# MoE 2 in two passes over the groups of weights, with seven products for all four blocks of tokens

## The chip, the cores and the metric

The kernel runs on one core of one Trainium2 chip. The metric is the device time of one execution in microseconds (us), as the median of three runs. Engines are named as in the profile: PE (TensorE), PEld (its weight loads), DVE (VectorE), ACT (ScalarE), POOL (GpSimd) and SP (SyncE, which issues most of the DMAs).

## The reference

Three stages, one after the other: attention with rotary embedding over 4 batches, 8 heads, 576 positions and 64 channels; a feed-forward stage with a clipped gate ("MoE 1"); a second one with a sigmoid gate ("MoE 2"). Both have 2304 tokens, 512 channels inside and out and 2048 hidden units. Their weights come as float64, all else as float32.

```python
attn = softmax(rotate(q) @ rotate(k).T / 8) @ v
x = attn.transpose(0, 2, 1, 3).reshape(2304, 512)
h = x @ w_in;  x = (h * clip(h + 3, 0, 6) / 6) @ w_out                 # MoE 1
h = x @ w_in2; out = (h / (1 + exp(-1.702 * h))) @ w_out2              # MoE 2
```

## The kernel before

Every matrix product is made of three: each float32 operand is split into a high part that the matmul's fp32r type holds and a low rest, and high x high, high x low and low x high are summed in PSUM. The splitting is a copy (`copy`, L399, most often on ACT) for the high part and a subtraction (`sub`, L389, on POOL or DVE) for the low one.

The order of all instructions is made by a planner (`Plan`, L81). `plan.op` (L94) notes an operation with its engine (and others that may take it), a cost, a key, and the buffers that it reads and writes. `plan.run` (L152) simulates the engines: whenever one is free it takes the ready operation with the lowest key whose buffers can be had, and the order that comes out is the order in which each engine's instructions stand in the program. Keys are thus priorities, spoken in planned time; an operation with a late key runs early if its engine has nothing else to do. The constants of the planner are in `C` (L31). On the chip every engine, SP's and POOL's DMA queues too, works its list in that order. The kernel calls `plan.run` three times: for attention with MoE 1 of batches 0 to 2 (L922), for the rest of MoE 1 and the start of MoE 2 (L954), and for MoE 2 (L1154).

Attention runs pair of heads by pair of heads (`pair`, L433), 16 in all. The probabilities are transposed on PE (L611) and split (L615, L632) for the product with v (L638). For some of them, as `full` (L417) says, the product is made in plain fp32 with v itself (L628), which saves the DVE's subtraction. MoE 1 of one batch (`moe1`, L766; 512 tokens, the last call also the 4 x 64 tail tokens) runs beside the attention of the next. Both feed-forward stages go over 8 groups of 256 hidden units (G = 2 slices of 128). The tokens form five blocks: 0 to 3 are the first 512 tokens of each batch, 4 holds the 256 tail tokens.

A group's weights are made by `weights` (L685). Kind "f64" loads pieces of 512 float64 per partition ("raw", two buffers), converts each to float32 ("cvt", two buffers) with one ACT instruction (L719), one POOL instruction (L721) and two DVE instructions (L725, L728), and splits it into high and low (wih, wil, woh, wol, two buffers each). In MoE 1 the first batch does this and stores the halves in DRAM ("keep", `w1_hl`), and the later batches load them through POOL's queue (kind "split", L695).

MoE 1's results of batches 0 to 2 go to DRAM (`y_dram`, L912) and come back near the end of MoE 1 (L934). Scaled by 1/6 they are split into yh and yl, one pair of buffers for each of the five blocks (L942 to L952).

MoE 2's order is `seq` (L962): per group the blocks 0, 2, 1, 3, 4, and behind each block's input products the output products of the block before. There are two forms of input products:

- "h" (L1016): per slice of 128 units 12 matmuls of 512 columns (256 for block 4), a sigmoid on ACT (L1033), a product on DVE (L1035), and the split into gh and gl.
- "w" (L1040), for blocks 0 and 1 from the second group on: units, channels and tokens are each cut in two, and seven products take the place of the eight products of halves, by sums of weight blocks (sh, sl; L736 to L758, made per group in buffers of the tags woh and wol) and of token blocks (th, tl; `ysums`, L986, once). The seven products are 42 matmuls of 256 columns (L1067) in four PSUM banks; one ACT copy (L1082) and four DVE additions (L1084 to L1090) recombine them into "hw" (one buffer), then sigmoid, product (L1103) and split.

"o" (L1107) are the output products of 128 tokens: six matmuls of 512 columns (L1139), added by DVE (L1143, L1145) into `oacc`, which holds all tokens; the last group's results are stored by SP (L1149; the tail's in halves, L1127). Weights of every group are converted from float64 within MoE 2 (L1010 to L1012).

## Time and profile before

| | before |
|---|---|
| median of three runs | 1136.02 us (1135.9 to 1136.06) |
| the profiled execution | 1136.14 us |
| span of the profiled execution, first to last instruction | 1134.3 us |
| granted TensorE clock, mean | 0.996 |
| PE / DVE / ACT / POOL busy | 97 / 63 / 49 / 57% of the span |

Times of stages, instructions and waits below are from the profiled execution. Starts are in us from its first instruction. A matmul's end is modelled, and matmuls overlap in the pipeline; its cost to the stream is the distance from its start to the next one's start. The profile writes "woh" for the sums' buffers too, since they share its tag, and w_hl for `w1_hl`.

### The profile page before, as it was taken

To read this page: it belongs to the slowest core of one execution; us is meant where nothing else is said; L and a number is where in the kernel's file an instruction comes from. 1 tells how busy PE (TensorE), PEld (TensorE's weight loads), DVE (VectorE), ACT (ScalarE), POOL (GpSimd) and SP (SyncE) were. 2 spreads that over 40 slices of the span, in tenths; PEclk is the share of its full clock that TensorE was granted. 3 is DMA by queue.
4 is the path that set the end of the run, shared out by engine and by line. 5 is a ranking of instruction groups with operands and counts; after the bars stand their busy time and mean duration, and the time that the engine had idled before them with its cause. 6 is when DMAs were issued, how large, how long until landed. Compare 5 with 4: busy or idle time off the path is not lost.

```text
span 1134.3 us, 16742 instructions
## 1 busy us (share of the span) xinstructions
PE 1098.7 (97%) x6264; PEld 898.2 (79%) x6264; DVE 713.2 (63%) x1092; ACT 558.9 (49%) x1133; POOL 645.3 (57%) x640
## 2 busy tenths in 40 slices
PE   5999999999999999999999999999999999999995
PEld 4666777777888888878887888888888888888884
DVE  5788777877656665566664544655655655566543
ACT  5788766666755564655556412444323433333330
POOL 5875876969563477363326435466645647455440
PEclk9999999999999999999999999999999999999998
DMA  3434565656543545443337543122102011120012
GB/s 92 129 129 142 160 225 165 212 183 206 171 130 111 153 151 181 120 141 107 112 112 260 157 140 85 66 74 75 42 34 75 19 56 37 39 74 21 19 75 93
DMA packets 58888, 129.69 MB, mean 114 GB/s; under 512 B 13752, under 2 KB 26808, under 8 KB 58040
## 3 DMA queue, kind: packets, MB, share of 16 engines
q1 hardware_dynamic: 44712, 78.13, 21.4%
q0 software_dynamic: 13824, 50.34, 14.7%
q8 instruction: 49, 0.80, 0.3%
q14 instruction: 31, 0.25, 0.1%
q10 hardware_dynamic: 272, 0.16, 0.0%
HBM read 103.97 MB, written 24.64 MB: 113 GB/s over the span
## 4 chain that ended last, share of the span: by engine, by line
PE 92%; DVE 5%; ACT 1%; issue 0%; DMA 0%; SPq 0%; DVEq 0%; ACTq 0%
PE psum L839 17%; PE psum L1139 17%; PE psum L814 17%; PE psum L1027 11%; PE psum L1067 6%; PE psum L611 6%; PE psum L558 5%; PE psum L638 4%; PE psum L628 3%; PE psum L598 1%; PE psum L545 1%; DVE sc L531 1%; DVE cvt L728 1%; PE psum L498 1%; PE psum L580 1%; PE psum L623 1%
## 5 line engine op out<-in xcount | busy, mean ns | idle before, releaser
L391 POOL TENSOR_TENSOR gl<-t,gh 128x512 fp32r<-128x512 f32 (+1 forms) x144 | 184.4, 1284 | 138.0 <-ACT gh L401 118.9
L533 ACT ACTIVATE P<-psum,sc 128x576 f32<-128x576 f32 x144 | 105.5, 739 | 60.4 <-DVE sc L531 60.0
L531 DVE TENSOR_REDUCE sc<-psum 128x1 f32<-128x576 f32 x144 | 102.6, 752 | 35.4 <-PE psum L558 31.8
L1145 DVE TENSOR_TENSOR oacc<-oacc,psum 128x512 f32<-128x512 f32 x124 | 85.0, 686 | 48.9 <-PE psum L1139 47.4
L615 ACT ACTIVATE PTh<-psum 128x512 fp32r<-128x512 f32 (+2 forms) x160 | 89.0, 598 | 49.3 <-PE psum L611 48.0
L1139 PE MATMUL psum<-woh,gh 128*128 128x512 f32 x284 | 111.2, 392 | 0.0
L1139 PE MATMUL psum<-woh,gl 128*128 128x512 f32 x284 | 110.8, 390 | 0.0
L1139 PE MATMUL psum<-wol,gh 128*128 128x512 f32 x284 | 110.7, 390 | 0.0
L401 ACT ACTIVATE gh<-t 128x512 fp32r<-128x512 f32 (+1 forms) x134 | 81.1, 607 | 53.3 <-DVE t L1035 25.7
L814 PE MATMUL psum<-xh,wih 128*128 128x512 f32 x256 | 105.7, 413 | 1.5 <-DVE t L821 1.2
L839 PE MATMUL psum<-gh,woh 128*128 128x512 f32 x256 | 104.3, 407 | 0.1
L848 DVE TENSOR_TENSOR y<-y,psum 128x512 f32<-128x512 f32 x112 | 76.4, 685 | 42.5 <-PE psum L839 41.7
L814 PE MATMUL psum<-xh,wil 128*128 128x512 f32 x256 | 100.5, 393 | 0.0
L839 PE MATMUL psum<-gh,wol 128*128 128x512 f32 x256 | 100.4, 392 | 0.0
L814 PE MATMUL psum<-xl,wih 128*128 128x512 f32 x256 | 100.3, 392 | 0.0
L839 PE MATMUL psum<-gl,woh 128*128 128x512 f32 x256 | 100.2, 391 | 0.0
L821 DVE SCALAR_TENSOR_TENSOR t<-t,psum 128x512 f32<-128x512 f32 (+1 forms) x80 | 50.0, 631 | 68.2 <-ACT t L819 68.0
L611 PE MATMUL psum<-ident,P 128*128 128x128 f32 (+1 forms) x640 | 87.9, 275 | 2.7 <-ACT P L533 1.2
L611 PEld LDWEIGHTS psum<-ident,P 128*128 128x128 f32 (+1 forms) x640 | 71.6, 135 | 23.6 <-issue 4.7
L819 ACT ACTIVATE t<-psum,three 128x512 f32<-128x512 f32 (+1 forms) x80 | 50.7, 644 | 79.8 <-PE psum L814 62.4
L1035 DVE TENSOR_TENSOR t<-t,psum 128x512 f32<-128x512 f32 (+1 forms) x52 | 31.5, 606 | 78.3 <-ACT t L1033 68.1
L632 DVE TENSOR_TENSOR PTl<-psum,PTh 128x512 fp32r<-128x512 f32 x92 | 61.5, 685 | 29.0 <-ACT PTh L615 28.7
(193 smaller groups left out, 2936.7 us busy)
## 6 DMA issues: line engine op xcount, KB each, us to landing
raw<-in_moe_w_in_dram SPq DMA_DIRECT2D x32, 512.0 KB, 3.8
raw<-in_moe_w_out_dram SPq DMA_DIRECT2D x32, 512.0 KB, 3.6
wih<-w_hl POOLq DMA_DIRECT2D x24, 512.0 KB, 4.4
wil<-w_hl POOLq DMA_DIRECT2D x24, 512.0 KB, 5.2
woh<-w_hl POOLq DMA_DIRECT2D x24, 512.0 KB, 4.4
wol<-w_hl POOLq DMA_DIRECT2D x24, 512.0 KB, 5.0
...
```

Source lines behind the costliest of these rows:

```text
L391: alts = [("Pool", ns or gps(n), lambda: nc.gpsimd.tensor_tensor(o(), i0(), i1(), op=op)), ("DVE", dve(n), lambda: nc.vector.tensor_tensor ...
L401: alts = {"ACT": ("ACT", act(n, psum), lambda: nc.scalar.activation(o(), i(), AF.Copy, scale=scale)), "DVE": ("DVE", dve(n, not psum), lam ...
L531: plan.op("DVE", dve(S), key + C["oM"], lambda: nc.vector.tensor_reduce(sc.t[:, i:i + 1], Sp.t[:, :, :HS], axis=AX.XY, op=ALU.max, negate= ...
L533: plan.op("ACT", act(S, True, True), key + C["oE"], lambda: nc.scalar.activation(halves(P[i].t), Sp.t[:, :, :HS], AF.Exp, bias=sc.t[:, i:i ...
L611: nc.tensor.transpose(T.t[:m, 0, c * 128:c * 128 + 128], P[hs + c].t[:, j * 128:j * 128 + m], ident)
L615: plan.op("ACT", act(512, True), key + C["oTh"], lambda T=T, hi=hi, m=m, fp=fp: nc.scalar.activation(hi.t.bitcast(F32) if fp else hi.t[:m] ...
L814: nc.tensor.matmul(hp.t[:, 0, :n], ww.t[:, cc, fs], xx.t[:, cc, :n], start=(cc == 0 and i == 0), stop=(cc == CC - 1 and i == 2))
L839: nc.tensor.matmul(yp.t[:, 0, :n], ww.t[:, a, cs], xx.t[:, a, :n], start=(i == 0), stop=(i == 3 * G - 1))
L848: plan.op("DVE", dve(n), ka + C["oY"], lambda yp=yp, y=y, c=c, n=n: nc.vector.tensor_tensor(y.t[:, c, :n], y.t[:, c, :n], yp.t[:, 0, :n], ...
L1027: nc.tensor.matmul(hp.t[:, 0, :n], ww.t[:, cc, fs], xx.t[:, cc, :n], start=(cc == 0 and i == 0), stop=(cc == CC - 1 and i == 2))
L1139: nc.tensor.matmul(op_.t[:, 0], xx.t[:, ts], ww.t[:, a, :], start=(i == 0), stop=(i == 3 * G - 1))
L1145: plan.op("DVE", dve(512), key, lambda op_=op_, tt=tt: nc.vector.tensor_tensor(oacc.t[:, tt], oacc.t[:, tt], op_.t[:, 0], op=ALU.add), r=[ ...
```

## The change

- **Two passes.** Pass 0 runs over all eight groups for the blocks 0, 1 and 4, pass 1 again over all groups for 2 and 3. Blocks 0 to 3 use the form "w" in every group, the first too; block 4 stays "h".
- **Operands.** Each of blocks 0 to 3 has seven prepared token operands in buffers of 7 x 512 (`prep`). Blocks 0 and 1 are prepared near the end of MoE 1; 2 and 3 within MoE 2 (`later`), 3 in block 0's buffers. y of batch 3 goes to DRAM too.
- **Weights.** Pass 0 makes the halves and the sums and stores all six in `w2_hl`; pass 1 loads them through POOL's queue. In pass 0 the sums have one pair of buffers (sh, sl); pass 1 alternates between these and block 4's.
- **Conversion.** The float64 conversion is moved out into `chunk`. For groups 0 to 4 (GZ = 5) it is planned into the first `plan.run`, in 20 chunks with keys Z0 + Z1 * i, and stored as float32 in `w2_f`; pass 0 loads these (kind "f32"). Groups 5 to 7 convert in pass 0 as before.
- **Buffers.** `oacc` is split by blocks, 2 and 3 reuse those of 0 and 1; hw has two buffers, gh2 and gl2 five each.
- **Order of the seven products** is 1, 2, 4, 6, 5, 7, 3 (before 1, 2, 6, 5, 7, 3, 4); the last store in two halves is block 3's last 128 tokens.
- **Constants.** F11 (unsplit products in batch 1, second head) goes from 3 to 2; keys of attention, MoE 1 and the planner's margins MA and MP change.

```diff
-C = {'T0': 59.504, 'D1': 12.604, 'LN1': 168.009, 'LN2': 130.306, 'LN3': 403.413, 'LM': 383.596, 'X': 32.498,
-     'K0': 3.856, 'RQ': 21.006, 'RK': 17.07, 'TQ': 1.889, 'TK': 1.171, 'V': 1.427, 'PB': 11, 'RT': 1.0, 'oM':
-     -0.122, 'oE': 0.391, 'REC': 1.0, 'TT': 1.191, 'TH': 0.258, 'TS': 0.034, 'PV': 1.449, 'PTB': 6, 'oTh':
-     0.144, 'oTl': -0.485, 'WL': 1.78, 'WS': 4.551, 'WS2': 1.346, 'MD': 8000, 'MA': 2000, 'MP': 400, 'YB':
-     1.149, 'YB0': -2.222, 'YS': 0.858, 'YT': -0.851, 'W2L': 22.0, 'W2S': 13.7, 'W2S2': -11.5, 'HC': 0.255,
-     'HD': -0.23, 'YD': 1.226, 'SPX': -9.638, 'F00': 3, 'F01': 1, 'F10': 2, 'F11': 3, 'F20': 0, 'F21': 0, 'G0':
-     5, 'T8': 0.572, 'P8': -1.224, 'SE': 1, 'MODE': 0.5, 'PORT': 8.0, 'oR': 0.2, 'oS': 1.092, 'oG': 9.844,
-     'oGl': -3.864, 'oY': -2.295, 'WC': -0.306}
+YBB = 1
+GZ = 5
+C = {'T0': 5.556, 'D1': 16.553, 'LN1': 168.009, 'LN2': 130.306, 'LN3': 403.413, 'LM': 383.596, 'X': 32.498,
+     'K0': 3.862, 'RQ': 18.769, 'RK': 18.355, 'TQ': 1.955, 'TK': 0.488, 'V': 1.136, 'PB': 11, 'RT': 1.0, 'oM':
+     -0.161, 'oE': 0.181, 'REC': 1.0, 'TT': 1.191, 'TH': 0.258, 'TS': 0.034, 'PV': 1.449, 'PTB': 6, 'oTh':
+     0.135, 'oTl': -0.478, 'WL': 1.803, 'WS': 4.642, 'WS2': 1.809, 'MD': 8000, 'MA': 8000, 'MP': 1000, 'YB':
+     1.048, 'YB0': -1.916, 'YS': 0.962, 'YT': 0.207, 'W2L': 22.0, 'W2S': 13.7, 'W2S2': -11.5, 'HC': 0.255, 'HD':
+     -0.141, 'YD': 1.283, 'SPX': -10.726, 'F00': 3, 'F01': 1, 'F10': 2, 'F11': 2, 'F20': 0, 'F21': 0, 'G0': 7,
+     'T8': 0.572, 'P8': -1.553, 'A0': 33.259, 'A1': 18.273, 'A2': 1.936, 'Z0': 406.045, 'Z1': 43.053, 'SE': 1,
+     'MODE': 0.5, 'PORT': 8.0, 'oR': 0.196, 'oS': 2.726, 'oG': 9.077, 'oGl': -6.999, 'oY': -3.913, 'WC': -0.237}
...
+    def chunk(nm, w, g, z, t_load, after=()):
...
+        return t
...
+                if sums and nm == "wi":
+                    d["sh"], d["sl"] = [Buf(plan, y3pool, x, [128, CC, 256], F32R, 1) for x in (("yh4", "yl4"), ("sh", "sl"))[g & 1]]
+                    for i, x in enumerate((d["sh"], d["sl"])):
+                        plan.op("Pool", 570, ts - 4, lambda x=x, o=(4 + i) * G * DM: nc.gpsimd.dma_start(
+                            flat(x.t), keep.t[g, :, o:o + G * DM]), r=[(keep, (g, "s", i))], w=[x], kb=512)
...
+                if kind == "f32":
+                    t = Buf(plan, wpool, "cvt", [128, CH], F32, 2)
+                    plan.op("SP", 475, t_load, lambda t=t, o=off + z: nc.sync.dma_start(t.t, w2_f.t[g, :, o:o + CH]),
+                            r=[(w2_f, (g, off + z))], w=[t], kb=256)
                 else:
+                    t = chunk(nm, w, g, z, t_load, after)
...
-                sh, sl = [Buf(plan, wpool, x, [128, G, DM], F32R, 2) for x in ("woh", "wol")]
+                sh, sl = [Buf(plan, y3pool, x, [128, CC, 256], F32R, 1) for x in ("sh", "sl")]
...
+                for i, x in enumerate((sh, sl)):
+                    plan.op("SP", 475, ts + 1, lambda x=x, o=(4 + i) * G * DM: nc.sync.dma_start(
+                        keep.t[g, :, o:o + G * DM], flat(x.t).bitcast(F32)), r=[x], w=[(keep, (g, "s", i))], kb=512)
...
         attention(apool, pp, gpool, wtile, tabs, xf_of, at)
+        for g in range(GZ):
+            for i, (nm, w, off) in enumerate((("wi", w_in2, 0), ("wo", w_out2, G * DM))):
+                for z in range(0, G * DM, CH):
+                    key = TA + C["Z0"] + C["Z1"] * (4 * g + 2 * i + z // CH)
+                    t = chunk(nm, w, g, z, key)
+                    plan.op("SP", 475, key + 4, lambda t=t, g=g, o=off + z: nc.sync.dma_start(w2_f.t[g, :, o:o + CH], t.t),
+                            r=[t], w=[(w2_f, (g, off + z))], kb=256)
...
+    yh, yl = [[Buf(plan, y3pool, f"{x}{i}", [128, 7, 512], F32R, 1) for i in range(2)] for x in ("yh", "yl")]
+    y4 = [Buf(plan, y3pool, x, [128, CC, 256], F32R, 1) for x in ("yh4", "yl4")]
+    def prep(src, dep, hi, lo, key):
...
-        wg = weights("f64", w_in2, w_out2, None, 0, tend - 25, tend - 12, tend - 5)
+        wg = weights("f32", w_in2, w_out2, w2_hl, 0, tend - 25, tend - 12, tend - 5, sums=True)
...
+    oaccs = [Buf(plan, opool, f"oacc{i}", [128, 4 if i != 2 else 2, DM], F32, 1) for i in (0, 1, 0, 1, 2)]
+    yh += [Buf(plan, opool, "yh2", [128, 7, 512], F32R, 1), Buf(plan, y3pool, "yh0", [128, 7, 512], F32R, 1)]
...
-    for g in range(NG):
-        for tb in (0, 2, 1, 3, 4):
-            if g and tb in WB:
-                seq.append(("w", g, tb))
-            else:
-                seq += [("h", g, tb, a) for a in range(G)]
+    for p, tbs in enumerate(((0, 1, 4), (2, 3))):
+        for g in range(NG):
+            for tb in tbs:
+                seq += [("w", p, g, tb)] if tb < 4 else [("h", p, g, tb, a) for a in range(G)]
+                if prev:
+                    seq += outs(prev)
+                prev = (p, g, tb)
...
+    for p in range(2):
+        for g in range(1 - p, NG):
+            ts = at[("w", p, g, 2 * p)]
+            if p:
+                ws[(p, g)] = weights("split", None, None, w2_hl, g, 0, ts - 10, ts - 5, 0, sums=True)
+            else:
+                ws[(p, g)] = weights("f32" if g < GZ else "f64", w_in2, w_out2, w2_hl, g, ts - C["A0"], ts - C["A1"], ts - C["A2"], sums=True)
...
+            if (p, g, tb) == (0, 2, 0):
+                later(2, key)
+            if (p, g, tb) == (1, 0, 2):
+                later(3, at[("w", 0, NG - 1, 1)] + 1)
```

## Rows read from the trace of the kernel before

**Rows 1.** The page: span, then each engine's busy time, share of the span, instructions.
```profile
span 1134.3 us, 16742 instructions
PE 1098.7 (97%) x6264; PEld 898.2 (79%) x6264; DVE 713.2 (63%) x1092; ACT 558.9 (49%) x1133; POOL 645.3 (57%) x640
```

**Rows 2.** Windows: us, each engine's busy time (instructions), granted PE clock, DMA share, GB/s.
```profile
0.00:110.00 110.00, 91.20 (x604) 63.31 (x605) 82.39 (x126) 79.87 (x179) 73.11 (x76) 1.00 0.40 124
200.00:225.00 25.00, 25.00 (x139) 19.53 (x137) 21.22 (x31) 14.99 (x30) 23.23 (x19) 1.00 0.62 211
250.00:590.00 340.00, 340.00 (x1996) 274.83 (x1995) 220.09 (x340) 193.36 (x403) 187.31 (x199) 1.00 0.46 139
780.00:1080.00 300.00, 300.00 (x1637) 259.72 (x1637) 180.32 (x274) 104.93 (x192) 165.06 (x153) 1.00 0.14 43
```

**Rows 3.** PE's timeline in MoE 2: start us, us, engine, line, what.
```profile
856.43 0.40 PE L1027 MATMUL psum<-yh,wih 128*128 128x512 f32 x1
...
862.03 0.40 PE L1139 MATMUL psum<-woh,gh 128*128 128x512 f32 x1
...
867.51 0.28 PE L1027 MATMUL psum<-yh,wih 128*128 128x256 f32 x1
...
870.31 0.39 PE L1139 MATMUL psum<-woh,gh 128*128 128x512 f32 x1
...
875.77 0.28 PE L1067 MATMUL psum<-yh,wih 128*128 128x256 f32 x1
...
880.75 0.40 PE L1139 MATMUL psum<-woh,gh 128*128 128x512 f32 x1
```

**Rows 4.** Timeline: PE's first matmul of MoE 2, DVE's last instruction of all.
```profile
731.34 0.51 PE L1027 MATMUL psum<-yh,wih 128*128 128x512 f32 x1
...
1121.86 0.42 DVE L1125 TENSOR_TENSOR oacc<-oacc,psum 128x256 f32<-128x256 f32 x1 [0.29 <-PE psum L1121]
```

**Rows 5.** PE's timeline in attention: a split product (two starts), unsplit ones.
```profile
269.81 0.39 PE L638 MATMUL psum<-PTh,vhl 128*128 128x512 f32 x1
270.04 0.39 PE L638 MATMUL psum<-PTl,vhl 128*128 128x512 f32 x1
...
270.36 1.93 PE L628 MATMUL psum<-PTh,rawv 128*64 128x512 f32 x4
```

**Rows 6.** Groups by line and shape, 725 to 1134: busy us, mean ns, idle before.
```profile
L391 POOL TENSOR_TENSOR gl<-t,gh 128x512 fp32r<-128x512 f32 x64 | 86.8, 1362 | 39.5 <-ACT gh L401 38.4 <-PE psum L1139 0.2
L1145 DVE TENSOR_TENSOR oacc<-oacc,psum 128x512 f32<-128x512 f32 x124 | 85.0, 686 | 48.9 <-PE psum L1139 47.4
L725 DVE SCALAR_TENSOR_TENSOR cvt<-cvt,raw 128x512 int32<-128x512 int32 x28 | 22.4, 800 | 7.4 <-POOL raw L721 6.2 <-ACT cvt L719 1.1
L392 DVE TENSOR_TENSOR t<-t,hw 128x512 f32<-128x512 f32 x28 | 22.3, 822 | 0.3 <-ACT t L1101 0.3
L728 DVE SCALAR_TENSOR_TENSOR cvt<-raw,cvt 128x512 int32<-128x512 int32 x28 | 20.4, 730 | 0.0
L721 POOL TENSOR_SCALAR raw<-raw 128x512 int32<-128x512 uint32 x28 | 18.6, 665 | 11.3 <-PE psum L1139 5.9 <-DMA raw<-in_moe_w_out_dram 3.7
L391 POOL TENSOR_TENSOR raw<-cvt 128x256 f32<-128x256 f32 x14 | 10.1, 738 | 11.3 <-DVE cvt L728 11.3
L1084 DVE TENSOR_TENSOR hw<-psum,hw 128x512 f32<-128x512 f32 x14 | 9.7, 692 | 10.4 <-PE psum L1067 10.2
```

**Rows 7.** One line's instructions: POOL's DMA issues, ns min/median/max.
```profile
L695 POOL DMA_DIRECT2D wih<-w_hl x24: 576/599/748, 146.4 to 681.9; - x24
```

**Rows 8.** Timeline after the last seven-product block: PE's next, POOL's low halves.
```profile
1093.98 0.40 PE L1139 MATMUL psum<-woh,gh 128*128 128x512 f32 x1
...
1097.66 2.55 POOL L391 TENSOR_TENSOR gl<-t,gh 128x512 fp32r<-128x512 f32 x2 [10.58 <-ACT gh L401]
```

**Rows 9.** Timeline: a POOL subtraction and the DVE conversion that starts under it.
```profile
896.86 1.30 POOL L391 TENSOR_TENSOR wil<-cvt,wih 128x512 fp32r<-128x512 f32 x1 [2.66 <-ACT wih L401]
...
897.51 1.20 DVE L725 SCALAR_TENSOR_TENSOR cvt<-cvt,raw 128x512 int32<-128x512 int32 x1
```

More of the change, by code (lines that the diff above doesn't have):

```diff
@@ L718, in weights @@
-                plan.op("SP", 475, t_load, load, w=[raw], kb=512, after=after)
-                plan.op("ACT", act(CH), t_load + C["WC"], lambda raw=raw, t=t: nc.scalar.activation(
-                    t.t, raw.t[:, :, 1].bitcast(F32), AF.Copy, scale=2.0 ** -112), r=[raw], w=[t])
-                plan.op("Pool", gps(CH, True), t_load + C["WC"], lambda raw=raw: nc.gpsimd.tensor_scalar(
-                    raw.t[:, :, 0], raw.t[:, :, 0].bitcast(U32), 2.0 ** -29 * (1 - 2.0 ** -7), -0.49, op0=ALU.mult, op1=ALU.add),
-                    w=[(raw, 0)], r=[raw], alts=[("DVE", 826, lambda raw=raw: nc.vector.tensor_scalar(
-                        raw.t[:, :, 0], raw.t[:, :, 0], 29, None, op0=ALU.logical_shift_right))])
@@ L935, in attention_moe_moe @@
                     r=[(y_dram, b)], w=[y], kb=1024)
-        ys += [y3, yt]
         copy(t0, CC * 256, lambda: flat(xt3[0].t), lambda: flat(xt.t), [xt], [xt3[0]])
@@ L1010, in attention_moe_moe @@
-    for g in range(1, NG):
-        ts = at[("w", g, 0)]
-        ws[g] = weights("f64", w_in2, w_out2, None, g, ts - C["W2L"], ts - C["W2S"], ts - C["W2S2"], sums=True)
+        pos += cost[e[0]]
+    ws = {(0, 0): wg}
+    for p in range(2):
[3 more added lines that the diff above has]
+                ws[(p, g)] = weights("split", None, None, w2_hl, g, 0, ts - 10, ts - 5, 0, sums=True)
+            else:
+                ws[(p, g)] = weights("f32" if g < GZ else "f64", w_in2, w_out2, w2_hl, g, ts - C["A0"], ts - C["A1"], ts - C["A2"], sums=True)
@@ new lines, in later @@
+    def later(tb, key):
+        rr = [Buf(plan, wpool, "raw", [128, CH, 2], I32, 2) for _ in range(2)]
+        for z, x in enumerate(rr):
+            plan.op("SP", 475, key - 6, lambda x=x, z=z: nc.sync.dma_start(
+                flat(x.t).bitcast(F32), y_dram.t[tb][:, 1024 * z:1024 * z + 1024]), r=[(y_dram, tb)], w=[x], kb=512)
+        prep(lambda c2, m: flat(rr[c2].t).bitcast(F32).rearrange("p (c t) -> p c t", c=2)[:, :, 256 * m:256 * m + 256],
+             lambda c2, m: (rr[c2], m), yh[tb], yl[tb], key)
@@ L1107, in attention_moe_moe @@
         else:
-            _, g, tb, r = e
-            d = ws[g]
-            tt = tb * 4 + r
-            if g == NG - 1 and tb == 4:
+            r = e[4]
+            tt, oacc = r, oaccs[tb]
+            if g == NG - 1 and tb == 3 and r == 3:
                 for m in range(2):
```

197 lines of the change are left out of this document (91 added, 106 removed).

## The prediction

> **What bounds the kernel now.** I read the page's busy line first, then the stages by windows, then TensorE's own timeline in MoE 2, and last the groups by line and shape for what the other engines do per group of weights. The page gives TensorE (PE) 1098.7 of 1134.3 us, VectorE (DVE) 63% and GpSimd (POOL) 57% [rows 1]. A busy PE need not be PE at its peak, so the windows and starts matter more. In the 300 us from 780 to 1080 PE is busy 300.00 us at the full granted clock (1.00, the 2.4 GHz level), while DVE has 180.32 and POOL 165.06 [rows 2]. The timeline shows the same without a modelled end: a matmul starts as soon as the one before lets it, block after block [rows 3]. So MoE 2 is bound by the number of columns that PE streams. Only the first 110 us have PE idle to speak of (91.20 of 110) [rows 2].
>
> From one start to the next, the blocks of MoE 2 cost on PE [rows 3]: an ordinary input product of 512 tokens ("h", 24 matmuls of 512 columns) 862.03 - 856.43 = 5.60 us; a seven-product block ("w", 42 matmuls of 256) 880.75 - 875.77 = 4.98; the 256-token tail ("h4") 870.31 - 867.51 = 2.80; the four output products of a block 5.47 (mean of 5.48 and 5.46), the tail's two half of that, 2.74.
>
> As proof: one group always has 2.80 + 4 x 5.47 + 2.74 = 27.42, eight have 219.4; before has 18 h blocks (four in group 0, two in each later one), 100.8, and 14 w blocks, 69.7. Together 389.9. The trace has 731.34 to 1121.86 = 390.5 [rows 4]. Nothing but column streaming is in that stage.
>
> **The products.** The change makes the 18 h blocks w blocks: 18 x (5.60 - 4.98) = **-11.2 us**, all of it on the path. The two passes themselves cost PE nothing: each (group, block) is still done once. Pass 0 (blocks 0, 1, tail) needs 2 x 4.98 + 2.80 + 2 x 5.47 + 2.74 = 26.4 us per group, pass 1 (blocks 2, 3) 2 x (4.98 + 5.47) = 20.9; eight of each are 378.6.
> The Trainium skill (TensorE: Matmul & The Clock Gate, Back-to-back issue gap) says that a sustained stream of weight-load-and-matmul pairs takes 131 ns at 512 columns and 81 ns at 128; with about 98 ns between them at 256 (an estimate from that page), w would cost 42 x 98 = 4.1 us against h's 24 x 131 = 3.1, and 18 swaps would lose 18 us. The starts speak against it: 5.60 us / 24 = 233 ns and 4.98 / 42 = 119 ns.
>
> **An edit in attention that rides along.** F11 goes from 3 to 2. In batch 1, second head, one probability block per pair of heads no longer goes through the unsplit fp32 product. That product takes two matmuls of 0.48 us (four in 1.93), the split one two starts 0.23 us apart, 0.46 for the pair [rows 5]. Four pairs: 4 x (0.96 - 0.46) = **-2.0 us** on PE, which is full there (25.00 of 25 at 200 to 225 [rows 2]); it adds four DVE subtractions, about 0.7 us each, to a DVE with 21.22 of 25 busy. Ends: 0 and -2.0. I take -2.0, as PE is the fuller one.
>
> **The twenty chunks beside attention.** Each adds 0.66 us on POOL, 0.80 + 0.73 on DVE [rows 6], one ScalarE (ACT) pass, a 512 KB load and a 256 KB store on SP. That is 31 us of DVE and 13 of POOL. They have late keys and share the two "raw" buffers with MoE 1's first conversions, so they fall mostly after about 250 us; from 250 to 590 DVE is idle for 120 us and POOL for 153 [rows 2], and this idle time hides them. If it isn't where it is needed, each chunk instruction can hold up a wanted one by up to 0.8 us. SP waits in order: a store that waits for DVE holds up the q, k and v loads behind it. No row prices that; all 20 chunks once late by 0.8 us would be 16 us if PE had no other work, none if it always has. I take **+1.0**, near zero, as DVE and POOL have a third of their time free.
>
> The constants T0, D1, RQ and others reorder attention. They add no work. Reordering could win back part of the 18.8 us that PE lacks in the first 110 us, or lose about as much; I take **0** and keep a fifth of it, 4 us, on both sides as an estimate for the range.
>
> **The new work in MoE 2.** Per pass-0 group I count POOL and DVE [rows 4, 6]. POOL: ten 512-wide subtractions (four gl, four weight lows, two sum lows) at 1.36, two tail ones and four sums at 0.74, four integer scalings at 0.66: 20.7 us with conversion, 18.1 without. DVE: six 512-wide adds at 0.69 and two half ones at 0.42 for the recombination, four products at 0.82, two of the tail at 0.42, ten output adds at 0.69, and four times 0.80 + 0.73 for conversion: 22.1 with, 16.0 without. Against 26.4 us this is DVE 84% and POOL 78% in the three groups that still convert (5 to 7), 61% and 69% in the other five. Pass 1 has no conversion: DVE about 14 and POOL 5.4 plus six weight-load issues of 0.60 [rows 7], 3.6, of 20.9.
> DMA: a converting group moves 2.1 MB in and 3.1 MB out (six kept halves of 0.52 MB), 5.2 MB in 26.4 us = 199 GB/s; others 159, pass 1 151. The stretch from 200 to 225 ran 211 GB/s with DVE at 85% and POOL at 93% and PE still at 25.00 of 25 [rows 2].
> So loads as high as these have been carried without a PE wait; the lower end is 0. The upper end is the shared-port sum of the first rival, 5.4. I take **+2.0**, nearer the row that was actually run.
>
> **Waits at the ends.** PE leaves the last w block of before at 1093.98, and POOL's last low half for it is ready at 1097.66 + 2.55 = 1100.21: 6.2 us [rows 8]. In the middle of a pass at least 2.74 + 4.98 = 7.7 us of other products lie between, and the tail's product can be pulled in. At the very end only block 2's outputs do, 5.47: PE waits **+0.8** (0 if DVE takes one of the two subtractions, 1.6 if they start one behind). At the pass switch, block 3's seven operands can be made only once block 0's last w is read; 2.74 + 4.98 + 5.47 + 2.80 + 5.47 + 4.98 + 2.74 = 29.2 us lie between, against seven DVE subtractions and four differences, some 10 us: nothing, or about 3 if they queue last. The final stores go from four half tiles to three whole and two half ones: nothing.
>
> **Sum.** 1134.3 - 11.2 - 2.0 + 1.0 + 0 + 2.0 + 0.8 = 1124.9 us of span. The profiled execution took 1136.14, 1.84 more than its span, and the median of the three runs is 0.12 below it: 1124.9 + 1.84 - 0.12 = **1126.6 us**. Own bounds: 1121 with the reordering's 4 and no waits in pass 0; 1131 with 4 the other way.
>
> **Rival 1: the converting groups run at the port's pace.** POOL and a DVE instruction with two SBUF inputs don't overlap: POOL's subtraction runs from 896.86 for 1.30 us, the DVE conversion that starts at 897.51 takes 1.20 instead of 0.69, ending 0.55 after POOL's [rows 9]. Sum both for a converting group at their unhindered 1.28 (two in 2.55 [rows 8]) and 0.69: POOL 10 x 1.28 + 6 x 0.74 + 4 x 0.66 = 19.9, DVE (four products, eight conversions) 8.3, together 28.2 against 26.4 us. That loses 1.8 in each of three groups, 5.4, where nothing moves to DVE's other side, and up to 5 each (15) if PE's outputs queue behind it. Against it: each subtraction moved to DVE frees 0.6 of the port, and DVE has 4 us left. With 8 us in place of my 2.0 it gives 1132.6, range 1130 to 1140.
> The Trainium skill (SBUF — State Buffer, Who interferes with whom) calls that pair of ports an exclusive lock, and says that the second one to issue blocks fully; the 1.20 us instruction agrees. By the lock alone the sum would be 1126.6 - 2.0 + 5.4 = 1130.0.
>
> **Rival 2, slower: the one pair of sum buffers.** In pass 0 the sums' halves (sh, sl) have one buffer. Group g+1's can be written only after block 1's products of group g, and PE needs them at the fourth product of the next group: 5.47 + 2.80 + 5.47 + 3 x 0.71 = 15.9 us later. The writing takes at least two POOL subtractions, 2 x 1.28 = 2.6 us (the ACT copy ahead of each not counted). It decides once more than 15.9 - 2.6 = 13.3 us of other work stands ahead of it on POOL. POOL's mean load gives 15.9 x 69% = 11.0 us in plain groups, 12.4 in converting ones. With POOL wholly full ahead of it, each of seven hand-overs loses 2.6 us, 18 in all: 1126.6 - 2.0 + 18 = 1143. The margin is 1 to 2 us, but the planner places these subtractions by key and not last; so I hold it unlikely.
>
> **Rival 3: w at h's price.** If seven products of one kind after another ran at 133 ns a matmul, w = h and nothing is gained: 1137.8. The 14 w blocks of before speak against it: the starts in them give 119 ns [rows 3].
> The Trainium skill's rule of 131 and 81 ns (same page and section) would go further and give 1126.6 + 11.2 + 18 = 1156 us; the same starts speak against it.
>
> **Chances.** Forecast 0.62, rival 1 0.22, rival 2 0.07, rival 3 0.01, the rule of 131 and 81 ns 0.01, an attention stage better by more than 4 us (below 1121) 0.07. Measurement can tell about 0.2%, 2.3 us: faster means below 1133.7. Faster: 0.62 + 0.07 + two thirds of rival 1 (0.14) = 0.83. Same: 0.08, rival 1's upper part and rival 3. Slower: 0.09. The range 1121 to 1136 leaves out 0.07 below and about 0.11 above.
>
> **What would show it.** Right: in MoE 2 all input products at 119 ns a matmul, first start to last about 381 us instead of 390.5, PE full in pass 1, a wait under 2 us before the last outputs. Rival 1: PE gaps and stretched DVE instructions in groups 4 to 6 of pass 0 alone. Rival 2: a PE gap at the fourth product of every group. Wrong from the start: MoE 2 beginning later than about 730 us, by attention reordered or SP held up; that would eat the gain before MoE 2 begins.

## The result, and the profile after

The changed kernel takes 1147.47 us (median of 4 runs, 1147.18 to 1149.14) where the kernel before takes 1135.96 beside it (4 runs, 1135.85 to 1136.06): 1.0103 times as long, 95% interval [1.009, 1.0115]. It was forecast at 1126.6 and is 11.5 us slower than before. Its profiled execution is the longest of the four, 1149.14, with a span of 1145.4.

Three points in the trace split a span: the first matmul of MoE 2, the end of the last matmul, and the end of the span.

| | before, us | after, us | difference |
|---|---|---|---|
| start to first matmul of MoE 2 | 731.3 | 759.2 | +27.8 |
| MoE 2 to the end of PE's last matmul | 390.5 | 382.8 | -7.7 |
| from there to the end of the span | 12.5 | 3.4 | -9.1 |
| span | 1134.3 | 1145.4 | +11.0 |

So MoE 2 is faster by about what was forecast, the end of the kernel has gained 9 us that were not forecast, and attention with MoE 1 has lost 28. The page after (against [rows 1]), PE's timeline at both ends of MoE 2 (against [rows 4]) and the windows of [rows 2], with the columns given there:

```profile
span 1145.4 us, 17756 instructions
PE 1097.4 (96%) x6582; PEld 913.2 (80%) x6582; DVE 808.8 (71%) x1197; ACT 579.1 (51%) x1176; POOL 655.9 (57%) x657
```

```profile
759.15 0.28 PE L1100 MATMUL psum<-yh,wih 128*128 128x256 f32 x1
759.27 0.28 PE L1100 MATMUL psum<-yl,wih 128*128 128x256 f32 x1
...
1141.67 0.28 PE L1148 MATMUL psum<-wol,gh 128*128 128x256 f32 x1
```

```profile
0.00:110.00 110.00, 88.53 (x568) 60.00 (x568) 81.06 (x124) 78.77 (x175) 75.23 (x79) 0.98 0.45 138
200.00:225.00 25.00, 24.71 (x131) 20.03 (x131) 20.67 (x31) 15.88 (x32) 23.75 (x20) 1.00 0.65 205
250.00:590.00 340.00, 324.66 (x1874) 261.56 (x1872) 264.73 (x374) 195.91 (x403) 185.12 (x192) 0.97 0.55 172
780.00:1080.00 300.00, 298.24 (x1879) 270.03 (x1878) 210.78 (x314) 111.78 (x213) 191.60 (x188) 1.00 0.55 185
```

MoE 2 (780 to 1080) is nearly as full as before, 298.24 of 300 us against 300.00, and its matmuls start 0.12 us apart. From 250 to 590 the kernel before had PE busy 340.00 of 340 at a granted clock of 1.00 [rows 2]; now it is 324.66 at 0.97. The idle 15.3 us are over half of the 28. The clock adds some 6 us: in three stretches at a granted 0.50, the 1.2 GHz level, PE is busy 12.24 us in all, and half of that is lost (an estimate from these windows):

```profile
293.50:300.30 6.80, 3.98 (x12) 2.92 (x13) 5.80 (x9) 2.79 (x7) 3.69 (x4) 0.50 0.82 257
426.60:433.40 6.80, 5.10 (x18) 4.27 (x19) 5.18 (x8) 1.03 (x2) 4.04 (x6) 0.50 0.48 120
477.80:481.20 3.40, 3.16 (x8) 2.48 (x8) 3.00 (x5) 3.02 (x8) 2.36 (x2) 0.50 0.78 283
```

From 250 to 590 DVE works 264.73 us instead of 220.09, 45 more, though the twenty chunks were counted at 31.

Where the time is lost shows in windows of that stretch, and then in the timeline at the worst of them (DVE, POOL, then ACT's and PE's next instructions):

```profile
275.00:300.00 25.00, 17.77 (x96) 12.46 (x95) 20.55 (x21) 12.29 (x27) 21.31 (x21) 0.87 0.71 234
...
425.00:450.00 25.00, 21.67 (x112) 17.87 (x113) 19.78 (x27) 11.63 (x22) 12.75 (x14) 0.86 0.52 153
475.00:500.00 25.00, 21.79 (x119) 17.90 (x120) 16.94 (x27) 17.12 (x34) 8.25 (x11) 0.93 0.47 148
```

```profile
285.62 0.69 DVE L868 TENSOR_TENSOR y<-y,psum 128x512 f32<-128x512 f32 x1
286.23 8.51 DVE L710 TENSOR_SCALAR raw<-raw 128x512 int32<-128x512 int32 x1
294.66 1.41 DVE L533 TENSOR_REDUCE sc<-psum 128x1 f32<-128x576 f32 x2
...
285.48 3.08 POOL L393 TENSOR_TENSOR t<-rawk,tab 128x640 f32<-128x640 f32 x2
288.52 1.25 POOL L393 TENSOR_TENSOR xl<-xf,xh 128x512 fp32r<-128x512 f32 x1
289.74 1.65 POOL L393 TENSOR_TENSOR roped<-t,t 128x320 f32<-128x320 f32 x2
291.34 0.59 POOL L730 DMA_DIRECT2D woh<-w_hl  x1
291.95 2.48 POOL L393 TENSOR_TENSOR xl<-xf,xh 128x512 fp32r<-128x512 f32 x2
...
295.44 0.74 ACT L535 ACTIVATE P<-psum,sc 128x576 f32<-128x576 f32 x1 [7.43 <-DVE sc L533]
...
296.32 0.42 PE L583 MATMUL psum<-ident,P 128*64 128x128 f32 x1 [7.22 <-ACT P L535]
296.72 0.79 PE L834 MATMUL psum<-xh,wih 128*128 128x512 f32 x1
```

L710 is the shift of a chunk, in the form that VectorE may run in POOL's place (the alternative of `chunk`). It normally takes 0.42 us. Here it starts at 286.23 while POOL goes from one two-tile instruction to the next, and ends at 294.74, when POOL's run ends (291.95 + 2.48 = 294.43). Behind it in DVE's order stand the softmax maxima (L533), behind those ACT's exponentials, behind those PE, which waits 7.22 us. After that PE runs at a lower clock: the slice has 0.87 granted, the mean of time at 2.4 and at 1.2 GHz, and the product of 512 columns at 296.72 is followed by the next 0.59 us later instead of 0.23. The same happens at 421.41 (the shift takes 6.25 us, PE waits 4.8) and at 469.60 (the next step of a chunk, L712, takes 4.93, PE waits 1.6).

Seventeen of the twenty shifts beside attention went to DVE; the planner's order decides that. The kernel shows why the planner sees no price in it: its model makes an instruction that is noted with `port` wait for the last one that has this note (L254, L279); the two-tile steps of a chunk have that note (L714, L717), the shift has none. The kernel before has the same alternative and used it twice, late, at 0.42 us each.

### The profile page after: what moved, and what is told of

Its sections match the earlier page's. It is cut to its first block, busy times and chain, and to the rows that moved or that the text cites. A ratio compares the mean times of both kernels' runs of the same rounds, so it can differ in the third digit from the quotient of the medians.

```text
span 1145.4 us, 17756 instructions
## 1 busy us (share of the span) xinstructions
PE 1097.4 (96%) x6582; PEld 913.2 (80%) x6582; DVE 808.8 (71%) x1197; ACT 579.1 (51%) x1176; POOL 655.9 (57%) x657
## 3 DMA queue, kind: packets, MB, share of 16 engines
q1 hardware_dynamic: 57268, 113.79, 30.2%
## 4 chain that ended last, share of the span: by engine, by line
PE 88%; DVE 6%; ACT 2%; issue 2%; DMA 1%; SPq 0%; POOL 0%; DVEq 0%; ACTq 0%; POOLq 0%
PE psum L859 17%; PE psum L1166 17%; PE psum L834 16%; PE psum L1100 13%; PE psum L613 6%; PE psum L560 4%; PE psum L640 4%; PE psum L630 2%; PE psum L1064 2%; PE psum L600 1%; DVE sc L533 1%; PE psum L547 1%; DVE cvt L712 1%; ACT P L535 1%; PE psum L513 1%
## 5 line engine op out<-in xcount | busy, mean ns | idle before, releaser
L533 DVE TENSOR_REDUCE sc<-psum 128x1 f32<-128x576 f32 x144 | 103.1, 751 | 28.1 <-PE psum L560 25.1
L403 ACT ACTIVATE gh<-t 128x512 fp32r<-128x512 f32 (+1 forms) x143 | 85.6, 606 | 50.8 <-DVE t L841 23.7
L613 PEld LDWEIGHTS psum<-ident,P 128*128 128x128 f32 (+1 forms) x640 | 74.0, 138 | 28.8 <-issue 6.9
L613 PE MATMUL psum<-ident,P 128*128 128x128 f32 (+1 forms) x640 | 90.5, 280 | 4.3 <-DVE PTl L634 1.5
L1129 ACT ACTIVATE t<-hw 128x512 f32<-128x512 f32 x64 | 37.2, 624 | 100.4 <-DVE hw L1118 100.4
L634 DVE TENSOR_TENSOR PTl<-psum,PTh 128x512 fp32r<-128x512 f32 x96 | 64.0, 684 | 28.5 <-ACT PTh L617 28.1
```

What stands on the lines that cost most here:

```text
L403: alts = {"ACT": ("ACT", act(n, psum), lambda: nc.scalar.activation(o(), i(), AF.Copy, scale=scale)), "DVE": ("DVE", dve(n, not psum), lam ...
L533: plan.op("DVE", dve(S), key + C["oM"], lambda: nc.vector.tensor_reduce(sc.t[:, i:i + 1], Sp.t[:, :, :HS], axis=AX.XY, op=ALU.max, negate= ...
L613: nc.tensor.transpose(T.t[:m, 0, c * 128:c * 128 + 128], P[hs + c].t[:, j * 128:j * 128 + m], ident)
```

## The experiments

The table has, for each run, MoE 2's first matmul, the time from there to the end of the last matmul, the rest of the span, and the waiting inside DVE's instructions before 745 us (summed over all: what a duration has above the median of the same line and shape). "Old constants" are those of the kernel before; "POOL only" means that the shifts of the twenty chunks have no alternative on VectorE.

| run | what is changed | MoE 2 starts | MoE 2 | rest | DVE waiting | median, us |
|---|---|---|---|---|---|---|
| before | | 731.3 | 390.5 | 12.5 | 21.8 | 1136.0 |
| after | | 759.2 | 382.8 | 3.4 | 54.7 | 1147.5 |
| e1 | after, shift in a two-tile form | 758.1 | 385.1 | 3.4 | 55.9 | 1151.5 |
| e5 | after, DVE's shifts left out | 746.7 | 385.2 | 3.4 | 41.4 | 1139.5 |
| e2 | after, POOL only | 738.9 | 382.7 | 3.4 | 31.1 | 1126.8 |
| e3 | after, no chunks beside attention | 733.0 | 424.7 | 4.0 | 22.2 | 1166.1 |
| e8 | after, chunks in MoE 1's last stage, POOL only | 733.2 | 457.9 | 5.0 | 24.1 | 1198.2 |
| e4 | before, constants of after | 734.7 | 390.4 | 13.0 | 21.5 | 1139.7 |
| e12 | before, F11 2 | 735.6 | 390.4 | 12.5 | 22.9 | 1140.2 |
| e17 | after, F11 3 | 761.9 | 382.8 | 3.4 | 52.0 | 1151.3 |
| e6 | e2, chunks from the ninth pair on | 748.0 | 382.8 | 3.5 | 31.8 | 1135.1 |
| e13 | e2, chunks from the third pair on | 746.6 | 382.8 | 3.9 | 32.0 | 1136.6 |
| e7 | e6, old constants, F11 2 | 739.3 | 381.1 | 4.3 | 31.0 | 1126.8 |
| e11 | e7, chunks one by one | 739.0 | 382.4 | 3.9 | 30.7 | 1127.4 |
| e10 | e11, eight chunks in MoE 1's last stage | 735.0 | 392.5 | 4.1 | 27.3 | 1133.4 |
| e14 | e13, old constants (F11 3) | 733.5 | 382.7 | 3.5 | 29.2 | **1120.6** |
| e15 | e14, alternative given back | 741.2 | 382.4 | 3.4 | 39.1 | 1127.4 |
| e16 | after, old constants (F11 3) | 744.5 | 380.8 | 4.4 | 40.1 | 1134.9 |
| e9 | before, tail first in the last group | 732.0 | 390.4 | 3.9 | 21.7 | 1127.6 |

### Is it the shift on VectorE?

e1 gives the shift another form:

```diff
-            w=[(raw, 0)], r=[raw], alts=[("DVE", 826, lambda raw=raw: nc.vector.tensor_scalar(
-                raw.t[:, :, 0], raw.t[:, :, 0], 29, None, op0=ALU.logical_shift_right))])
+            w=[(raw, 0)], r=[raw], alts=[("DVE", 826, lambda raw=raw: nc.vector.scalar_tensor_tensor(
+                raw.t[:, :, 0], raw.t[:, :, 0], 29, zero.broadcast_to([128, CH]), op0=ALU.logical_shift_right, op1=ALU.bitwise_or))])
```

> The plan and the order of every engine stay as in the changed kernel; only the form of the chunk's shift on VectorE is another: a scalar_tensor_tensor with a zero tile (two inputs) in place of the tensor_scalar (one input). Theory A (the one-input shift on VectorE waits for a whole run of back-to-back GpSimd instructions, 8.51 us at 286.2 and 6.25 us at 421.4, and what stands behind it in VectorE's order waits with it): if only the one-input form waits like this, MoE 2 starts at 737 to 742 instead of 759.3 and the time is about 1127 to 1131 us; if the two-input form waits just as long, MoE 2 still starts after 755 and the long shifts are seen again, 5 us or more each. Theory B (the reordered keys of attention and MoE 1 alone cost the 28 us) and theory C (the stores of the chunks hold up SP's queue): MoE 2 starts after 755, the time is 1145 to 1149, and the shifts are short.

The order is the same, and so is the wait: the timeline and the line's instructions (ns, min/median/max) of e1.

```profile
284.37 8.77 DVE L712 SCALAR_TENSOR_TENSOR raw<-raw,zero 128x512 int32<-128x512 int32 x1
```

```profile
L712 DVE SCALAR_TENSOR_TENSOR raw<-raw,zero x17: 674/685/8768, 284.4 to 495.7; 128x512 int32<-128x512 int32 x17
```

8.77 us is 8.51 and the 0.26 by which this form is longer anyway (0.685 against 0.423). Both forms wait alike at this place beside POOL's run; both read and write SBUF alone. VectorE's additions that take one input from PSUM, as the one just before the shift, don't wait (after, ns min/median/max):

```profile
L868 DVE TENSOR_TENSOR y<-y,psum x112: 669/687/691, 159.6 to 756.5; 128x512 f32<-128x512 f32 x112
```

e5 keeps the order and leaves the shifts out; e2 takes the choice away from the planner.

```diff
(e5)
+        left = []
...
-            w=[(raw, 0)], r=[raw], alts=[("DVE", 826, lambda raw=raw: nc.vector.tensor_scalar(
-                raw.t[:, :, 0], raw.t[:, :, 0], 29, None, op0=ALU.logical_shift_right))])
+            w=[(raw, 0)], r=[raw], alts=[("DVE", 826, lambda left=left: left.append(1))])
...
-            t.t.bitcast(I32), t.t.bitcast(I32), 3, raw.t[:, :, 0], op0=ALU.logical_shift_left, op1=ALU.bitwise_or),
+            t.t.bitcast(I32), t.t.bitcast(I32), 3, zero.broadcast_to([128, CH]) if left else raw.t[:, :, 0], op0=ALU.logical_shift_left, op1=ALU.bitwise_or),
(e2)
-            w=[(raw, 0)], r=[raw], alts=[("DVE", 826, lambda raw=raw: nc.vector.tensor_scalar(
+            w=[(raw, 0)], r=[raw], alts=() if pool else [("DVE", 826, lambda raw=raw: nc.vector.tensor_scalar(
...
-                    t = chunk(nm, w, g, z, key)
+                    t = chunk(nm, w, g, z, key, pool=True)
```

> The order of every engine is that of the changed kernel, but the shifts that VectorE would run are left out (17 of the 20 beside attention; their next instruction takes a zero tile in place of the shifted words, so the three lowest bits of these weights are missing). This tells the wait of the shift from the order of the plan. Theory A (it is these shifts, waiting 8.5 and 6.3 us for GpSimd): MoE 2 starts at 738 to 744 and the time is 1126 to 1132. Theory A2 (any two-tile VectorE instruction of SBUF that stands at these places waits as long, so that the next one in order takes the wait): MoE 2 starts at 750 or later. Theory D (the new order that the planner chose around them is itself bad): after 755, with no long VectorE instruction.

> The shifts of the twenty chunks beside attention have no alternative on VectorE; they run on GpSimd alone, and the planner orders the rest anew. Theory A (the shifts on VectorE wait for GpSimd): no VectorE instruction of a chunk lasts over 2 us, MoE 2 starts at 735 to 742 (4 to 6 us of the front end stay), the time is 1125 to 1131 us. Theory B (the new keys): MoE 2 starts after 755 and the time is 1145 or more. Theory C (SP's queue): the same as B. If the two-input instructions of the chunks (4.93 us at 469.6) wait as badly, something between: 745 to 752.

Without the shifts, in the same order, MoE 2 starts 12.4 us earlier, between the two readings (738 to 744, and 750 or later). The chunk's next step, a two-tile instruction, now falls into the same run of POOL's and takes the wait over (e5's timeline):

```profile
286.09 5.03 DVE L714 SCALAR_TENSOR_TENSOR cvt<-cvt,zero 128x512 int32<-128x512 int32 x1
```

With all shifts on POOL, and the order that the planner then makes (e2), the start is 20.2 us earlier, no step of a chunk takes over 1.93 us, and the kernel takes 1126.77 us, 0.9918 [0.989, 0.9947] of before. 12.4 of these 20 us go with the shifts alone (e5), the rest with the steps that still wait there and with the new order. So Theory A holds in its wider form: a VectorE instruction between SBUF tiles that starts under a run of POOL's may wait for the whole run.

The Trainium skill (SBUF — State Buffer, Who interferes with whom) has this as an exclusive lock, and says that the order of issue, not the form of the instruction, decides who blocks. e1 against the changed kernel, two forms in one place, agrees with that. "For the whole instruction" is the length that the page gives; 8.51 us is seven POOL instructions and a DMA issue. Other shifts waited only for the one that was running (1.62 us at 342.21, under one that ends at 343.54). What decides between the two is open.

### Do the chunks have to lie beside attention?

e3 sets `GZ = 0` (group 0's kind to match), so that all eight groups are converted in pass 0. e8 moves the loop over the chunks, POOL only, behind MoE 1's `next(last)`, with keys spread over its last stage.

```diff
(e3)
-GZ = 5
+GZ = 0
(e8)
...
+                    key = tend - 0.9 * C["LM"] * (1 - (4 * g + 2 * i + z // CH) / 20)
+                    t = chunk(nm, w, g, z, key, pool=True)
```

> No group is converted beside attention; all eight are converted in pass 0 of MoE 2. Keys of attention and MoE 1 as in the changed kernel. Theory A or C (the chunks and their stores delay attention): MoE 2 starts at 733 to 738, and what it then takes tells the price of converting in pass 0, 383 us if it is hidden (time about 1123), 400 or more if VectorE and GpSimd don't keep up. Theory B (the new keys delay attention): MoE 2 still starts after 755.

> The twenty chunks are converted not beside attention but in the last stage of MoE 1 (after 603 us), their shifts on GpSimd alone; keys otherwise those of the changed kernel. In that stage VectorE is 55% and GpSimd 43% busy. Twenty chunks add 31 us of VectorE and 13 us of GpSimd to its 136 us. If idle time hides them there: MoE 2 starts at 733 to 736 (as without any chunks, 733.2) and the time is 1120 to 1122. If the waits of the two engines for each other, or SP's queue with its 40 transfers, reach TensorE: MoE 2 starts at 738 or later.

e3 starts MoE 2 at 733.0, but needs 424.7 us for it: five more converting groups cost 42 us, some 8 each, while the three of the changed kernel cost nothing that shows. PE's waits in that stage add up to 30 us, for DVE, ACT and POOL in turn, 5.6 at the longest; some 9 more go with the clock (half of PE's 17.7 busy us at a granted 0.50, an estimate). What makes these waits isn't shown: from 733 to 960 the waiting inside DVE's instructions, counted as in the table, is 24.0 us against 20.3 in the changed kernel. Its windows, in which PE is idle and the clock falls though DVE is 91% busy at most:

```profile
775.00:800.00 25.00, 22.77 (x136) 19.71 (x135) 17.75 (x27) 9.15 (x17) 19.52 (x18) 1.00 0.56 203
800.00:825.00 25.00, 22.20 (x108) 18.36 (x107) 22.78 (x28) 12.81 (x23) 20.05 (x17) 0.86 0.53 159
825.00:850.00 25.00, 15.91 (x117) 14.29 (x115) 19.16 (x26) 10.23 (x21) 15.86 (x16) 0.89 0.46 137
```

e8 also starts early (733.2), as expected, but the twenty chunks take until 788 us, some 9 us each (why so long wasn't followed), and group 0's weights come behind them: 1198.2 us, which neither reading gave. Its longest waits of PE:

```profile
PE psum L1100 <- ACT wih L403: 45.8, 1, 45.8
PE psum L1166 <- ACT hw L1110: 2.9, 2, 2.8
```

### The constants and F11

e4 is the kernel before with all constants of the changed one; e12 changes F11 alone; e17 puts F11 back in the changed kernel.

```diff
(e12)
-'F11': 3
+'F11': 2
(e17)
-'F11': 2
+'F11': 3
```

> The kernel before with the constants of the changed kernel, with its own MoE 2. Theory B (the new keys of attention and MoE 1 cost the 28 us): MoE 2 starts after 755 and the time is about 1160 us. Theories A and C: MoE 2 starts at 731 to 736 (the first four pairs of heads 4 to 5 us late, the third stage of MoE 1 2 us shorter) and the time is 1134 to 1142 us. MoE 2 of the kernel before is not expected to move.

> The kernel before with F11 2 instead of 3 and nothing else. The forecast put this at -2.0 us: MoE 2 from 729.3, 1134.2 us. If the runs with old keys and F11 2 were late through it (their ninth pair started 2 to 3 us later than in the kernel before): MoE 2 from 733 to 735 and 1138 to 1140 us; the new keys then cost 1 us or nothing by themselves. If it is neutral: 1136, and the new keys cost the 3.4 us.

> The changed kernel with F11 3 instead of 2. By itself F11 2 cost the kernel before 3.6 us. If that is all it does here: MoE 2 from 755 to 757, 1143 to 1145 us. If its extra VectorE work is what crowded the shifts into GpSimd's runs: MoE 2 well below 750 and 1120 to 1135 us, the long shifts gone.

F11 2 alone makes MoE 2 start 4.2 us later and the kernel take 1140.15, 1.0031 [1.002, 1.0043] of before. All constants together cost 3.4 in the kernel before, so the reordering without F11 is about neutral there. Beside the chunks F11 is not what matters: e17 has shifts of 5.80 and 6.30 us on DVE and starts even later, which neither reading gave.

### The front, and where a chunk may start

The planner also put three chunks into the first 42 us. SP's queue, e2 (first two lines) against e3:

```profile
8.00 0.35 SPq L933 DMA_DIRECT2D w_f<-cvt  x1
8.39 0.43 SPq L459 DMA_DIRECT2D rawv<-in_v_dram  x1
```

```profile
3.79 0.59 SPq L459 DMA_DIRECT2D rawv<-in_v_dram  x1
```

The first store waits for its chunk until 8.00 and holds up the first load of V; the second pair of heads starts at 34.9 in e2, 29.7 in e3. e6, e13 and e14 hold the loads back with the planner's `after`; e7 is e6 with the old constants, and e10 and e11 spread the chunks out.

```diff
(e6, e7)
+                    t = chunk(nm, w, g, z, key, [steps[len(steps) // 2]], pool=True)
(e13, e14)
+                    t = chunk(nm, w, g, z, key, [steps[len(steps) // 8]], pool=True)
(e11; e10 the same for 12 chunks, and 8 in the last stage)
+                    kk = 4 * g + 2 * i + z // CH
+                    t = chunk(nm, w, g, z, key, [steps[int(len(steps) * (0.22 + 0.72 * kk / (4 * GZ)))]], pool=True)
(e15)
-                    t = chunk(nm, w, g, z, key, [steps[len(steps) // 8]], pool=True)
+                    t = chunk(nm, w, g, z, key, [steps[len(steps) // 8]])
```

> Shifts of the twenty chunks on GpSimd alone, and no chunk loaded before the ninth pair of heads; in the kernel that had only the first of these edits three chunks ran between 0 and 42 us and the first store held up attention's first load of V on SP's queue (8.39 against 3.79 us without chunks). Theory C2 (that queue costs the front 4 to 5 us): the second pair of heads starts at 29 to 31 us (34.9 there), MoE 2 at 733 to 735 (739.2 there), the time is 1121 to 1123. If the chunks cost their 6 us wherever they lie: MoE 2 at 738 to 740, 1126 to 1128. If three more chunks in the crowded second half cost more than the front gains: later than 741.

> The run with the shifts on GpSimd alone, and no chunk loaded before the third pair of heads, new keys. If the front is what the chunks cost there: second pair at 30 us instead of 34.9, MoE 2 from 734 to 736 (739.2 there), 1121 to 1123 us. If the order that the planner then chooses again puts a two-tile VectorE instruction beside a run of GpSimd (5.31 us at 292.81 with the chunks after the ninth pair): a later start, 740 to 748, with that instruction to be seen.

Both win the front back (second pair at 30.2 and 30.5) and lose more later: MoE 2 starts at 748.0 and 746.6, the last reading of each. The order that follows puts attention's own subtraction for V on DVE under a run of POOL's; PE waits 5.5 us for what stands behind it (e13, timeline and waits):

```profile
293.23 5.29 DVE L394 TENSOR_TENSOR vhl<-rawv,vhl 128x640 fp32r<-128x640 f32 x1
```

```profile
PE psum L640 <- DVE PTh L621: 5.5, 1, 5.5
```

> As the run with late chunks, and the constants of attention and MoE 1 of the kernel before (F11 stays 2). Theory B2 (the new keys cost 3.4 us, as the kernel before with the new constants showed, 734.7 against 731.3): MoE 2 starts 3 to 4 us earlier than in the run with late chunks, at 729 to 732, time 1118 to 1120. If the old keys were good only without chunks: no earlier, or later.

> As the run with late chunks and old keys (MoE 2 from 739.5, 1126.8 us), but the twenty chunks are released one by one over the pairs of heads from the first quarter on, instead of all after the ninth pair, where a VectorE instruction waited 4.34 us for GpSimd at 293.55. If it is the crowd of chunks that makes the waits: no VectorE instruction of attention over 3 us, MoE 2 from 734 to 737, 1121 to 1124 us. If each chunk costs the same anywhere: 739 again and 1126 to 1127.

> Constants of attention of the kernel before (F11 2), shifts on GpSimd alone; twelve chunks (groups 0 to 2) spread evenly over the pairs of heads, one every 0.06 of attention from its first quarter on, and eight (groups 3 and 4) in the last stage of MoE 1, where the run that put all twenty there began MoE 2 at 733.4 but then waited 45.8 us for group 0. If what costs attention its 6 to 8 us is chunks meeting GpSimd's runs, fewer and spaced ones cost about half: MoE 2 starts at 733 to 736, the time is 1120 to 1123. If a chunk costs the same wherever it lies in attention (0.3 to 0.4 us each): 735. If the last stage can't hold eight: a wait of PE on weights of group 3 or 4 in MoE 2, and a time over 1127.

The old constants take 8.7 us off e6's start, more than the 3 to 4 expected. With them and F11 2 the same instruction takes 4.3 us in all three, however the chunks are spaced (MoE 2 starts 0.3 us apart in e7 and e11): it isn't the crowd of chunks. e10 starts MoE 2 at 735.0, and then loses 10 us around the switch of passes, where PE waits some 6 us in all (885 to 960), 2.0 at a time at most, and has a clock of 0.86 from 935 to 960.

> As the run beside it, with all constants of attention and MoE 1 of the kernel before (F11 3). If the old keys are 3.4 us better with chunks too: MoE 2 from 731 to 734, 1118 to 1121 us. If the gain was F11 or is lost to the chunks: 735 to 740, 1123 to 1127.

> The run with old keys and no chunk before the third pair (MoE 2 from 733.5, 1120.6 us), in which the shifts beside attention may again go to VectorE. Theory A (the choice of engine is the cause): some shifts run on VectorE, at least one lasts over 4 us, MoE 2 starts at 745 to 755 and the time is 1132 to 1142. If the old constants keep the shifts away from GpSimd's runs: under 740 and 1120 to 1127, with short shifts.

> The changed kernel with the constants of attention and MoE 1 of the kernel before (F11 3) and nothing else. Theory A: shifts on VectorE wait as in the changed kernel; MoE 2 from 748 to 757, 1135 to 1145 us (some 4 us of it F11). Theory B (the constants): MoE 2 from 736 to 738 (the front's 4 us stay), 1122 to 1126.

e14 takes **1120.59 us, 0.9858 [0.9841, 0.9874] of before**, and beats both kernels, as its first reading said. Its chunks cost attention 2.1 us (733.5 against 731.3). Its page and windows:

```profile
span 1119.7 us, 17756 instructions
```

```profile
250.00:590.00 340.00, 337.74 (x1981) 273.18 (x1980) 246.09 (x378) 203.23 (x422) 203.20 (x218) 1.00 0.60 183
```

DVE and POOL have the same chunks to do as in the changed kernel, and PE loses 2.3 us of 340 instead of 15.3. e15 is e14 with the choice given back: all twenty shifts go to DVE, MoE 2 starts 7.7 us later and the time is 1127.41, which neither reading gave. That no shift lasts over 1.97 us there was not expected; the order that comes with them has attention's V subtraction take 5.88 us instead, under these of POOL's:

```profile
371.09 5.88 DVE L394 TENSOR_TENSOR vhl<-rawv,vhl 128x640 fp32r<-128x640 f32 x1
...
373.79 1.25 POOL L393 TENSOR_TENSOR gl<-t,gh 128x512 fp32r<-128x512 f32 x1
375.00 0.60 POOL L730 DMA_DIRECT2D woh<-w_hl  x1
375.59 0.54 POOL L730 DMA_DIRECT2D wol<-w_hl  x1
376.11 0.55 POOL L730 DMA_DIRECT2D wil<-w_hl  x1
```

It ends at 376.97, 1.93 us after the last tensor instruction of that run, though it takes 0.81 us where nothing holds it (after, 303.73); so here POOL's DMA issues seem to hold it too. e16 adds three chunks at the front: MoE 2 starts 3.3 us later than in e15, between its two expectations. So the alternative, with the order that it brings, costs 20.2 us with the new constants and 7.7 with the old ones (there with no chunk before the third pair): the mechanism is one, its price is what the order makes of it. The eight runs of e16 lie between 1129.3 and 1142.2, and its profiled execution, 1131.74, is among the shorter; why one order gives such different times wasn't traced.

### The last stores

e9 is the kernel before, with its last group alone taking the tail first.

```diff
-        for tb in (0, 2, 1, 3, 4):
+        for tb in (0, 2, 1, 3, 4) if g < NG - 1 else (4, 0, 2, 1, 3):
```

> The kernel before, whose last group alone takes the 256-token tail first instead of last. In the trace of before 12.4 us pass between the last VectorE instruction (1121.86 + 0.42) and the end of the span, in which the stores of the tail move 47 to 49 GB/s with one in ten of the DMA engines' time used; in the changed kernel, where the last stores are those of block 3, it is 3.4 us. Theory E (the tail's stores, issued last, cost those 9 us, and the change gained them by its order of blocks): the end lies 3 to 4 us behind the last VectorE instruction and the time is 1126 to 1129 us. Theory F (the drain is a property of that kernel's many stores, or of the output as a whole): still 10 us or more, 1135 to 1137.

1127.56 us, 0.9923 [0.9909, 0.9938]; 3.9 us remain behind the last matmul, as Theory E said. (In before 12.4 us pass from the start of DVE's last instruction to the end of the span, 12.1 from its end.) Windows of that rest, before and then e9 (DMA share and GB/s are the last two columns):

```profile
1122.00:1134.00 12.00, 0.00 (x0) 0.00 (x0) 0.28 (x1) 0.00 (x0) 0.00 (x0) 0.63 0.12 42
```

```profile
1122.40:1126.30 3.90, 0.02 (x1) 0.00 (x0) 0.69 (x1) 0.00 (x0) 0.00 (x0) 1.00 0.36 134
```

In before the rest is spent on the tail's stores alone, at 0.12 of 16 DMA engines (1.9 of them) and 42 GB/s. The tail's rows go to `out[2r:2r+2, 512:576]`, two batches at a time. The Trainium skill (DMA: Bandwidth & Descriptors, Why a DMA increments its semaphore by 16 and not by 1) says that a transfer is spread over the largest number of engines, up to 16, that divides the slowest dimension of both its sides; by that rule two batches on one side give 2. The measured share agrees; no run stored the tail in another shape. In the changed kernel the tail is done in pass 0, and its stores lie beside matmuls.

## Why the prediction was wrong, point by point

- **What was seen and not.** The forecast was 1126.6, the result 1147.5. That e2 takes 1126.8 is chance: there two errors, +8.6 at the start of MoE 2 (738.9 against 730.3) and -9.1 at the end, cancel.
- **The products, right.** 382.1 us were forecast for MoE 2 to its last outputs (390.5 - 11.2 + 2.0 + 0.8), 382.8 measured, in ten of the runs within 2 us.
- **"The twenty chunks beside attention", +1.0: the step that failed.** It counted one POOL shift of 0.66 and two DVE steps, and read the idle thirds of DVE and POOL as cover. It left out that the shift has an alternative on VectorE, which both kernels show (L710 after, L723 before), and it let an instruction hold up a wanted one "by up to 0.8 us". One held it up for 8.51. The 27.8 us add up in three runs: constants 3.4 (e4, 734.7), chunks with their shifts on POOL 4.2 (e2, 738.9), the choice of DVE with the order that it brings 20.2 (after, 759.2). So the chunks cost 24.4 in place of 1.0; against e3, the changed kernel without them (733.0), it is 26.2. With another order the same twenty cost 2.1 (e14). What they cost is not their work but which of attention's instructions wait behind theirs.
- **The clock, left out.** A PE gap of 7 us was followed by a stretch at half the clock. About 6 of the 28 us are this, by PE's 12.24 busy us at a granted 0.50.
- **F11, -2.0: wrong in sign.** It was worked out as PE time alone, with PE full; measured it is +4.2 (e12). The four added DVE subtractions, noted and priced at nothing, stand between PE's products on an engine that was 85% busy there. Up to 735 us PE is idle 3.3 us longer in e12 than in before (busy 708.57 against 711.90), 1.6 of it from 265 to 300, where a two-tile subtraction of MoE 1 (xl) on DVE takes 2.96 us under two of POOL's (277.08). So the order that the planner makes anew has its part; how the 6 us between forecast and result add up isn't shown.
- **The reordered keys, 0:** -0.8 by e4 and e12 together. Right in the kernel before, and inside the 4 of the range. Beside the chunks it was not: there the old keys, with F11 2 in both, start MoE 2 8.7 us earlier (e7 against e6).
- **SP's queue**, named as a danger without a price: the three chunks that hold it up cost 3.3 us (e16 against e15, one profiled execution each) at the very front, where the chunks were not expected at all: their late keys don't keep them back when SP and a buffer are free.
- **"The final stores: nothing", wrong by 9.1 us.** Their number was looked at, not their shape, and the 12.4 us from the start of DVE's last instruction to the end of the span [rows 1, 4] were not asked about. 8.7 of the 9.1 come with the order of the blocks alone (e9).
- **The rivals.** Rival 1 had the mechanism, POOL and DVE in each other's way on SBUF, but placed it in pass 0, with a price per instruction overlapped. There three converting groups cost nothing that shows; eight cost 42 us (e3), by which mechanism isn't shown. Rival 2 and 3 did not occur: PE waited 0.9 us at most in MoE 2, and its starts stay 0.12 us apart. The Trainium skill's rule of 131 and 81 ns (TensorE: Matmul & The Clock Gate, Back-to-back issue gap) doesn't hold here either. What was named as the sign of a wrong start, MoE 2 later than 730 us, is what happened.
